# Fourth layer of a four-layer decode step with gradients: resident transposes dealt out between arriving w1 tiles and into two normalisations, twelve zero stores moved to the end

## The chip, the cores and the metric

The kernel runs on one core of a Trainium2 chip. The metric is device time in microseconds (us) of one execution. Engines are named as in the profile: PE (TensorE matmul), PEld (TensorE weight load), DVE (VectorE), ACT (ScalarE), POOL (GpSimd), SP (SyncE, which here only issues DMAs).

## The reference

One token of width 1024 passes four residual layers: attention (A), dense block (B), attention, dense block; A and B have the same weights both times. The outputs are the result of the forward pass and the gradients of all inputs.

```python
def _A_ref(x, k_cache, v_cache, wq, wo):          # 32 query heads, 4 key/value heads, width 128
    W = min(4096, max(256, Sk // 4))              # the last 4096 of 32768 positions
    q = (x @ wq) ...
    k = repeat(k_cache[:, :, Sk - W:, :]); v = repeat(v_cache[:, :, Sk - W:, :])
    p = softmax(q k * Dh ** -0.5)
    return (p v) @ wo

def _B_ref(x, w1, b1, w2):                        # 1024 -> 3584 -> 1024
    h = x @ w1 + b1
    return (h * tanh(softplus(h))) @ w2

x = x + _A_ref(_layernorm(x), ...)
x = x + _B_ref(_layernorm(x), ...)
x = x + _A_ref(_layernorm(x), ...)
x = x + _B_ref(_layernorm(x), ...)
...
_out, _vjp = jax.vjp(_f, A_x, A_k_cache, A_v_cache, A_wq, A_wo, B_w1, B_b1, B_w2)
return (_out, *_vjp(grad_out))
```

The gradients of the two caches have the full 32768 positions, and all but the last 4096 are zero. Writing those zeros is most of the kernel's output: 112 pieces of 128 x 2048 bf16, 0.5 MB each.

## The kernel before

**Stages.** The order of the program is `attn_fwd` (A1), `mlp_B2_fwd`, `attn_fwd` (A3), `mlp_B4`, `ln_bwd`, `attn_bwd` (A3), `mlp_B2_bwd`, `attn_bwd` (A1) and the output jobs. `mlp_B4` is the fourth layer; it does forward and backward in one pass, since the gradient of its output is given. In the profiled execution the layers begin at about 0, 70, 114 and 147 us, the backward of the third at 225, that of the second at 256, that of the first at 306, and the first weight gradients are stored from 329 us on.

**What stays in SBUF.** wq, wo, K and V are loaded once. The forward pass needs them one way round and the backward pass the other way, so each piece of 128 x 1024 has to be transposed in place: eight 128 x 128 transposes on TensorE (L254) into a PSUM bank of the pool `pt` (three banks), then one copy by VectorE or ScalarE (`evac`, L228 and L230; a running estimate of each engine's load picks the engine). Such a piece is a *unit*; there are 88 of them (32 wq, 8 K, 16 V, 32 wo). `unit` lists one as soon as the forward pass is done with it, `fill(n)` transposes the next `n` of the list in the order wo, V, K, wq, and `fill_kind` finishes all of a kind before the product that needs them. Where the fills stand in the program is written out by hand: the lists `F_` of the attention layers, `FB4` of the fourth layer.

**What is streamed.** w1 and w2 pass through rings of SBUF slots. `queue` is the order of all loads; `rel` returns a slot and `pump` issues the next loads that have one. All these loads and all stores but some small ones go through SP's queue, in program order, with eight transfers under way at most. In the third and fourth layer the ring `r4` has four slots, which lie in the half of K that is free after the third layer's scores; they hold one block of w1.

**The fourth layer.** w1 is worked in four blocks of 1024 columns (the last of 512). Block `b` goes through `fwd(b)` (the products of the normalised input with each w1 tile of 0.5 MB as it arrives, into the PSUM tile `big`), one fill, `sel(b)` (column sums, L670), `act(b)` (the activation and its derivative, some fifteen small VectorE operations on 128 x 8), `turn(b)` (the block's own tiles are transposed in place) and `bwd(b)` (products of the hidden gradient with them into `R`; then `rel` of the slots, which issues the next block's loads). Then come the block's zero stores, `zeros(ZB4[b])`, and twelve fills. The next block's first product waits for its tile.

```python
        for b in range(4):
            fwd(b)
            fill(FB4[b][0])
            sel(b)
            act(b)
            turn(b, 0, 8 if b < 3 else 4)
            fill(FB4[b][1])
            bwd(b)
            ...
            zeros(ZB4[b])
            fill(FB4[b][2])
```

**Zero stores.** `zeros(n)` issues the next `n` pieces from a tile of zeros on SP's queue; they wait for nothing but the queue. Before: 4 in the second layer, 33 in the third, 38 in the fourth, 11 and 4 in the backward of the third and second, 7 before the backward of the first, 8 in it, and 7 among the output jobs.

**Output stage.** Weight gradients are outer products of pairs of rows (PE, L237), copied from PSUM to staging tiles of 0.5 MB (DVE L863, ACT L866) and stored from there by SP. There are seven such tiles in turn (nine from the wo jobs on). Jobs are listed by `add(kind, n, f, z)`, where `z` zero stores follow the job: seven pairs of w2 columns, sixteen w1 jobs with the K and V gradients between them, then wo and wq.

Of the kernel before, what the change touches and what calls it, by code (L numbers as in the profile page):

```python
# [14 lines left out]
P = 128  # L15
# [6 lines left out]
def kernel(  # L22
# [22 lines left out]
    nc = tc.nc  # L45
# [202 lines left out]
    def bc(col, n=32):  # L248
        return col.to_broadcast([P, n])
# [17 lines left out]
    def fill(n):  # L267
        for _ in range(min(n, len(units))):
            u = units.pop(0)[2]
            T8(nat_blocks(u), u)  # L270

    def fill_kind(kind):
        fill(sum(u[0] <= rank[kind] for u in units))

# [49 lines left out]
                wt[name] = (1, n, kt([P, wk_n.get(name, n)], FP32, name)[:])  # L324
        return wt[name][2][:, 0:n]

    def ln_fwd(x_col, l):
        xx = wk("xx", 2 * TD)
        nc.vector.tensor_copy(xx[:, 0:TD], x_col[:])
        nc.vector.tensor_mul(xx[:, TD:], x_col[:], x_col[:])  # L330
        sps = sm_tile(P, 2 * TD)
        mm(sps[:], bc(oneD[:, 0:1], P), xx[:], True, True)
        s12 = wk("s12", 2)
        nc.vector.reduce_sum(s12[:], sps[:].rearrange("p (a b) -> p a b", a=2), axis=AX.X)
        var = wk("var", 1)
        nc.vector.scalar_tensor_tensor(out=var[:], in0=s12[:, 0:1], scalar=s12[:, 0:1], in1=s12[:, 1:2],
                                       op0=ALU.mult, op1=ALU.subtract, reverse1=True)
        lnv = wk("lnv", 1)
        nc.scalar.activation(lnv[:], var[:], ACT.Ln, bias=eps_t[:, 0:1], scale=1.0)
        rstd = wk(f"rstd_{l}", 1)  # L340
        nc.scalar.activation(rstd[:], lnv[:], ACT.Exp, scale=-0.5)
        n_bf = npair[:, LI[l], :]
        nc.vector.tensor_scalar(out=n_bf, in0=x_col[:], scalar1=s12[:, 0:1], scalar2=rstd[:, 0:1], op0=ALU.subtract, op1=ALU.mult)
        n32 = kt([P, TD], FP32, f"n32_{l}")
        last = nc.vector.tensor_scalar(out=n32[:], in0=x_col[:], scalar1=s12[:, 0:1], scalar2=rstd[:, 0:1], op0=ALU.subtract, op1=ALU.mult)
        return dict(n32=n32, rstd=rstd, l=l), n_bf, last

    def ln_bwd(tt, sv, g_col, nxt, hook=None):

        n32, rstd = sv["n32"], sv["rstd"]  # L350
        nc.vector.tensor_mul(tt[:, TD:], tt[:, 0:TD], n32[:])
        if hook:
            hook()
        sps = sm_tile(P, 2 * TD)
        mm(sps[:], bc(oneD[:, 0:1], P), tt[:], True, True)
        ab = wk("s12", 2)
        nc.vector.reduce_sum(ab[:], sps[:].rearrange("p (a b) -> p a b", a=2), axis=AX.X)  # L357
        t2 = wk("t2", TD)
        nc.vector.scalar_tensor_tensor(out=t2[:], in0=n32[:], scalar=ab[:, 1:2], in1=tt[:, 0:TD],
                                       op0=ALU.mult, op1=ALU.subtract, reverse1=True)  # L360
        gx = wk("gx", TD)
        nc.vector.tensor_scalar(out=gx[:], in0=t2[:], scalar1=ab[:, 0:1], scalar2=rstd[:, 0:1], op0=ALU.subtract, op1=ALU.mult)
        g_new = kt([P, TD], FP32, f"g_{nxt}")
        g_bf = kt([P, TD], BF16, "gb_X0")[:] if nxt == "X0" else gpair[:, LI[nxt], :]
        nc.vector.tensor_add(g_bf, g_col[:], gx[:])
        last = nc.vector.tensor_add(g_new[:], g_col[:], gx[:])
        return g_new, g_bf, last


# [266 lines left out]
        return x_new, sv, da4  # L636

    def mlp_B4(x_col, da4):
        sv, n_bf, g0 = ln_fwd(x_col, "B4")
        dh = kt([P, TF], FP32, "dh_B4")  # L640
        sv["dh"] = dh
        R = one_tile("R", 512)
        big = one_tile("big", 1024)
        blk, hcol = {}, {}

        def fwd(b):
            full = b < 3
            nh, nt, nch = (2, 2, 4) if full else (1, 4, 2)
            hb = big[:, (b % 2) * 512:(b % 2 + 1) * 512]
            blk[b] = [take(("w1b", b, i)) for i in range(nch)]  # L650
            for i in range(nch):
                w = blk[b][i][0]
                for ti in range(nt):
                    t = nt * i + ti
                    for n in range(nh):
                        g = 2 * n + ti if full else ti
                        mm(hb[32 * g:32 * g + 32, :], bc(n_bf[:, t:t + 1]), w[:, ti, n * 512:(n + 1) * 512],
                           i == 0, i == nch - 1, tile_position=(0, 32 * g))
            evac(jkf[:, :], hb, 512, "D")

        def sel(b):
            full = b < 3
            nh, nk = (2, 8) if full else (1, 4)
            hps = sm_tile(P, 8)
            for cc in range(2):
                for tt in range(2):
                    k = 2 * cc + tt
                    mm(hps[:, k:k + 4 * (nh - 1) + 1:4], jkf[:, cc * 256 + tt:cc * 256 + tt + 255:2], selD[:] if full else sel1[:], k == 0, k == 3)
            h = wk("h", nk)
            nc.vector.tensor_add(h[:], hps[:, 0:nk], b1_f[:, 8 * b:8 * b + nk])  # L670
            hcol[b] = h

        def act(b):
            nk, f0 = 8 if b < 3 else 4, 8 * b
            dact = wk("dact", nk)
            mish(hcol[b][:], apair[:, 0, f0:f0 + nk], dact[:], nk)
            nc.vector.tensor_mul(hpair[:, 0, f0:f0 + nk], da4[:, f0:f0 + nk], dact[:])
            nc.vector.tensor_mul(dh[:, f0:f0 + nk], da4[:, f0:f0 + nk], dact[:])
            spent(2.8, 0.2)

        def turn(b, lo, hi):
            for u in range(lo, hi):
                if b < 3:
                    w = blk[b][u // 2][0][:, u % 2, :]
                    T8([w[:, (k // 2) * 256 + k % 2:(k // 2) * 256 + k % 2 + 255:2] for k in range(8)], w)
                else:
                    w = blk[b][u // 2][0][:, 2 * (u % 2):2 * (u % 2) + 2, :]
                    T8([w[:, q, (k // 2) * 256 + k % 2:(k // 2) * 256 + k % 2 + 255:2] for q in range(2) for k in range(4)],
                       w.rearrange("p t f -> p (t f)"))

        def bwd(b):
            nk, f0 = 8 if b < 3 else 4, 8 * b
            for k in range(nk):
                for tp in range(4):
                    w = blk[b][tp][0][:, 0:2, :] if b < 3 else blk[b][tp // 2][0][:, 2 * (tp % 2):2 * (tp % 2) + 2, :]
                    mm(R[32 * tp:32 * tp + 32, 0:256].rearrange("p (t d) -> p t d", t=2), bc(hpair[:, 0, f0 + k:f0 + k + 1]),
                       w[:, :, k * P:(k + 1) * P], b == 0 and k == 0, b == 3 and k == nk - 1, tile_position=(0, 32 * tp))
            for _, ring, i in blk.pop(b):
                rel(ring, i)
# [9 lines that stand above are left out]
            if b == 3:  # L709
                zsrc[:] = [None, 1024]  # L710
            zeros(ZB4[b])
            fill(FB4[b][2])
        evac(jkf[:, 0:256], R[:, 0:256], 256, "D")
        dn = sm_tile(P, TD)
        for i in range(2):
            mm(dn[:].rearrange("p (a i) -> p i a", i=2)[:, i, :], jkf[:, i * P:(i + 1) * P], ident_f[:, 0:P:32], i == 0, i == 1)
        tt = wk("xx", 2 * TD)
        nc.vector.tensor_copy(tt[:, 0:TD], dn[:])
        return tt, sv
# [282 lines left out]
    def wo_dead():  # L1002
# [42 lines left out]

        for n in range(NW2 // 2):
            add("w2a", n, lambda c=2 * n: pair_half(row_sp["w2"], c, w2_out, w2_lhs, 0))
            add("w2", n, lambda c=2 * n: pair_half(row_sp["w2"], c, w2_out, w2_lhs, 1), {0: 1, 2: 2, 6: 1}.get(n, 0))
        for n in range(16):
            add("w1", n, lambda t=n // 2, hf=n % 2: w1_job(t, hf), n < 3)  # L1050
            add("kv", n, lambda n=n: kv_step(n))
        for n in range(HQ // 8):
            add("wo", n, lambda c=4 * n: tall_jobs(row_sp["wo"], range(c, c + 4), wo_out, wo_lhs))
# [24 lines left out]
    def out_step(i):  # L1078
        if i == 0:
            nc.scalar.copy(z8.bitcast(FP32), zlo[:, 0:2].bitcast(FP32).to_broadcast([P, 2048]))  # L1080
            zsrc[:] = [z8, 4096]
            zeros(8)
        elif i < 3:
            rows_turn(row_sp["w2"], i - 1, w2_sp[i - 1], "rep")
        elif i > 2:
            run_jobs(1 if i == 4 else 2)

    ZB4 = [11, 10, 10, 7]
    FB4 = [(1, 0, 12), (1, 0, 12), (1, 0, 12), (1, 8, 0)]

    pump()
    x1, sA1 = attn_fwd(x0, "A1", True, sA, [0] * 6, [0] * 4)
    x2, sB2, da4 = mlp_B2_fwd(x1)
    x3, sA3 = attn_fwd(x2, "A3", False, sB, [4, 2, 8, 2, 2, 2], [10, 4, 19])
    tt, sB4 = mlp_B4(x3, da4)
    g3, g3b, _ = ln_bwd(tt, sB4, gcol, "A3")
    g2, g2b, _ = attn_bwd(g3, g3b, "A3", sA3, False, "B2", [4, 3, 5, 2], [5, 1, 5], lambda i: None)
    (g1, g1b, _), x4_bf = mlp_B2_bwd(g2, g2b, sB2, x3)
    zeros(7)
    g0, g0b, _ = attn_bwd(g1, g1b, "A1", sA1, True, "X0", [0] * 4, [0, 0, 0], out_step)  # L1100
    assert not queue and not held and not units
    order[:] = ["op", "big0", "big1", "op", "acc", "R", "op", "sm"]
# [37 lines left out]
```

## Time and profile before

| | us |
|---|---|
| three runs | 445.44, 449.69, 450.57 |
| median | 449.69 |
| span of the profiled execution | 446.6 |

| | busy, us | share of the span |
|---|---|---|
| PE | 329.8 | 74% |
| PEld | 195.8 | 44% |
| DVE | 234.5 | 53% |
| ACT | 220.7 | 49% |
| POOL | 14.7 | 3% |
| SP's DMA queue, as a share of 16 engines | | 96.9% |

169.45 MB are moved (70.00 MB read and 98.84 MB written), 379 GB/s on the mean over the span.

How to read what is shown below. The slices cut the span into 40 parts of 11.2 us; digits are tenths, 9 being 90% or more. PEclk is the clock that TensorE was granted, in tenths of full speed. In the table by stretches each row has the stretch, its length, the busy time and number of instructions of PE, PEld, DVE, ACT and POOL, the granted clock, the DMA share (1.02 to 1.05 where all engines are busy throughout) and GB/s. In the order of time each row has the start, the duration, engine and line, output and inputs, and in brackets the idle time of the engine before it and what ended that. The line of a matmul is mostly that of the helper `mm` (L237), so rows are told apart by their tiles. Landing is the end of a DMA's transfer as its semaphore shows it. A busy share of PE says little by itself, since matmuls are pipelined.

### The profile page before, as it was taken

To read this page: it belongs to the slowest core of one execution; us is meant where nothing else is said; L and a number is where in the kernel's file an instruction comes from. 1 tells how busy PE (TensorE), PEld (TensorE's weight loads), DVE (VectorE), ACT (ScalarE), POOL (GpSimd) and SP (SyncE) were. 2 spreads that over 40 slices of the span, in tenths; PEclk is the share of its full clock that TensorE was granted. 3 is DMA by queue.
4 is the path that set the end of the run, shared out by engine and by line. 5 is a ranking of instruction groups with operands and counts; after the bars stand their busy time and mean duration, and the time that the engine had idled before them with its cause. 6 is when DMAs were issued, how large, how long until landed. Compare 5 with 4: busy or idle time off the path is not lost. (4 is left out here: it accounts for less than half of the span.)

```text
span 446.6 us, 9185 instructions
## 1 busy us (share of the span) xinstructions
PE 329.8 (74%) x3732; PEld 195.8 (44%) x3732; DVE 234.5 (53%) x532; ACT 220.7 (49%) x335; POOL 14.7 (3%) x52
## 2 busy tenths in 40 slices
PE   3486645487778886879878788887589889987770
PEld 1164215355455774858756555773322312221110
DVE  2045102097253452535645378572256888888871
ACT  1045000056173452736724267571457678898881
POOL 1000000000000000000000000000400020000000
PEclk9998655579899796978999989666865555555555
DMA  8999999999999999998999999999998699999997
GB/s 328 423 420 418 409 410 379 401 336 328 365 398 406 417 404 381 341 376 290 381 412 405 374 412 336 383 333 358 415 397 356 280 397 403 371 386 413 408 411 319
DMA packets 49143, 169.45 MB, mean 379 GB/s; under 512 B 4784, under 2 KB 5836, under 8 KB 44876
## 3 DMA queue, kind: packets, MB, share of 16 engines
q1 hardware_dynamic: 48784, 168.31, 96.9%
q8 instruction: 29, 0.48, 0.4%
q0 software_dynamic: 256, 0.54, 0.3%
q14 instruction: 14, 0.11, 0.1%
q10 hardware_dynamic: 60, 0.01, 0.0%
HBM read 70.00 MB, written 98.84 MB: 378 GB/s over the span
## 5 line engine op out<-in xcount | busy, mean ns | idle before, releaser
L230 ACT COPY K<-tp 128x1024 bf16<-128x1024 bf16 x58 | 57.3, 1015 | 18.1 <-PE tp L254 16.9
L254 PE MATMUL tp<-ident_bf,K 128*128 128x128 bf16 x656 | 58.3, 258 | 4.8 <-DMA K<-in_B_w_dram 1.7
L237 PE MATMUL op<-wo 2*128 2x512 bf16 (+2 forms) x123 | 56.0, 566 | 2.3 <-ACT V L866 0.7
L254 PEld LDWEIGHTS <-K 128*128 128x128 bf16 x656 | 50.9, 119 | 11.0 <-issue 8.0
L237 PEld LDWEIGHTS <-wo 128*128 128x128 bf16 (+2 forms) x590 | 22.5, 101 | 65.8 <-issue 56.3
L230 ACT COPY wo<-tp 128x1024 bf16<-128x1024 bf16 x32 | 32.6, 1026 | 29.5 <-PE tp L254 27.2
L237 PE MATMUL big<-wo 2*128 2x512 bf16 x82 | 27.5, 590 | 10.2 <-DVE wo L863 4.0
L866 ACT CAST wo<-op 128x512 bf16<-128x512 f32 (+1 forms) x51 | 29.3, 592 | 5.5 <-PE big L237 2.0
L863 DVE CAST wo<-big 128x512 bf16<-128x512 f32 x31 | 21.1, 686 | 11.5 <-ACT wo L866 6.9
L568 DVE CUSTOM_DVE_ANT_0 K<-K,kp 128x1024 bf16<-128x1024 bf16 (+1 forms) x22 | 24.3, 1126 | 5.3 <-PE R L237 2.3
L254 PE MATMUL tp<-ident_bf,wo 128*128 128x128 bf16 x352 | 26.4, 230 | 0.3 <-ACT wo L230 0.2
L866 ACT CAST wo<-big 128x512 bf16<-128x512 f32 x35 | 20.7, 601 | 11.3 <-DVE wo L863 5.8
L228 DVE COPY jk<-R 128x512 f32<-128x512 f32 (+1 forms) x11 | 7.3, 664 | 33.7 <-PE R L237 33.7
L254 PEld LDWEIGHTS <-wo 128*128 128x128 bf16 x352 | 21.7, 102 | 7.2 <-issue 6.4
L237 PE MATMUL acc<-wo 2*128 2x512 bf16 (+1 forms) x41 | 24.3, 592 | 0.0
L230 ACT CAST jk<-big 128x512 bf16<-128x512 f32 x4 | 2.6, 659 | 42.1 <-DVE jk L228 42.1
L228 DVE COPY K<-tp 128x1024 bf16<-128x1024 bf16 x24 | 16.3, 690 | 11.3 <-PE tp L254 11.2
L237 PE MATMUL big<-wq,npair 128*32 128x512 bf16 x128 | 13.4, 553 | 10.0 <-DMA wq<-in_A_wq_dram 8.6
L237 PE MATMUL sm<-wo 2*128 2x512 bf16 (+1 forms) x33 | 19.9, 604 | 1.1 <-DVE cols L357 1.1
L863 DVE CAST wo<-op 128x512 bf16<-128x512 f32 (+1 forms) x32 | 18.4, 600 | 4.1 <-PE big L237 2.0
L237 PE MATMUL R<-wo 2*128 2x512 bf16 (+1 forms) x33 | 19.7, 596 | 0.0
L228 DVE CAST jk<-big 128x512 bf16<-128x512 f32 x4 | 2.8, 712 | 30.9 <-PE big L237 30.9
(269 smaller groups left out, 591.7 us busy)
## 6 DMA issues: line engine op xcount, KB each, us to landing
out_dram<-misc SPq DMA_DIRECT2D x97, 512.0 KB, 10.3
out_dram<-wo SPq DMA_DIRECT2D x37, 512.0 KB, 4.9
K<-in_B_w_dram SPq DMA_DIRECT2D x28, 512.0 KB, 6.9
K<-in_A_k_cache_dram SPq DMA_DIRECT2D x9, 1024.0 KB, 20.5
wq<-in_A_wq_dram SPq DMA_DIRECT2D x8, 1024.0 KB, 10.1
out_dram<-wq SPq DMA_DIRECT2D x8, 1024.0 KB, 8.0
K<-in_B_w_dram SPq DMA_DIRECT2D x16, 448.0 KB, 5.0
out_dram<-wo SPq DMA_DIRECT2D x16, 448.0 KB, 5.1
```

The lines of the kernel that those rows point to most:

```text
L228: return nc.vector.tensor_copy(out_ap, in_ap)
L230: return nc.scalar.copy(out_ap, in_ap)
L237: return nc.tensor.matmul(out_ap, lhsT=lhsT, rhs=rhs, start=start, stop=stop, skip_group_check=True, **kw)
L254: nc.tensor.transpose(ps[:, b * P:(b + 1) * P], ap, ident_bf[:])
L568: return nc.vector.tensor_tensor_reduce(out=w, in0=w, in1=vec, scale=1.0, scalar=0.0, op0=ALU.mult, op1=ALU.add, accum_out=acc_col)
L863: nc.vector.tensor_copy(out_ap, in_ap)
L866: nc.scalar.copy(out_ap, in_ap)
```

## The change

The fills of the fourth layer are dealt out otherwise: `FT4[b][i]` of them stand before the products of block `b`'s tile `i`, and the twelve behind each block go. `fill_ahead(n)` puts the transposes of `n` units into PSUM at a point where the statistics of a normalisation have just been issued to TensorE, and `fill_land` copies them out after the normalisation's vector chain; this is used in the fourth layer's forward and backward normalisation. The third layer has one fill fewer in its first place; the fourth has 45 (with the two normalisations) instead of 48, so four wq units more are left for `fill_kind("wq")` in the third layer's backward pass. Twelve zero stores are moved: five fewer in the third layer, seven fewer in the fourth, three more ahead of the first layer's backward pass, two more in it, four more among the w2 jobs and three more among the w1 jobs.

```diff
+    ahead = []
+
+    def fill_ahead(n):
+        for _ in range(min(n, len(units), 3 - len(ahead))):
+            u, ps = units.pop(0)[2], ptile()
+            for b, ap in enumerate(nat_blocks(u)):
+                nc.tensor.transpose(ps[:, b * P:(b + 1) * P], ap, ident_bf[:])
+            ahead.append((u, ps))
+
+    def fill_land():
+        while ahead:
+            u, ps = ahead.pop(0)
+            evac(u, ps[:])
...
-    def ln_fwd(x_col, l):
+    def ln_fwd(x_col, l, nfill=0):
...
         mm(sps[:], bc(oneD[:, 0:1], P), xx[:], True, True)
+        fill_ahead(nfill)
...
         last = nc.vector.tensor_scalar(out=n32[:], ...)
+        fill_land()
...
-    def ln_bwd(tt, sv, g_col, nxt, hook=None):
+    def ln_bwd(tt, sv, g_col, nxt, hook=None, nfill=0):
...
         mm(sps[:], bc(oneD[:, 0:1], P), tt[:], True, True)
+        fill_ahead(nfill)
...
         last = nc.vector.tensor_add(g_new[:], g_col[:], gx[:])
+        fill_land()
...
-        sv, n_bf, g0 = ln_fwd(x_col, "B4")
+        sv, n_bf, g0 = ln_fwd(x_col, "B4", 2)
...
             for i in range(nch):
+                fill(FT4[b][i])
                 w = blk[b][i][0]
...
             zeros(ZB4[b])
-            fill(FB4[b][2])
...
-            add("w2", n, ..., {0: 1, 2: 2, 6: 1}.get(n, 0))
+            add("w2", n, ..., (1, 1, 2, 1, 1, 1, 1)[n])
...
-            add("w1", n, lambda t=n // 2, hf=n % 2: w1_job(t, hf), n < 3)
+            add("w1", n, lambda t=n // 2, hf=n % 2: w1_job(t, hf), n < 4 or n in (7, 9))
...
-            zeros(8)
+            zeros(10)
...
-    ZB4 = [11, 10, 10, 7]
-    FB4 = [(1, 0, 12), (1, 0, 12), (1, 0, 12), (1, 8, 0)]
+    ZB4 = [8, 8, 8, 7]
+    FT4 = [(0, 0, 0, 0), (6, 2, 2, 2), (6, 2, 2, 2), (5, 4)]
+    FB4 = [(1, 0), (1, 0), (1, 0), (1, 4)]
...
-    x3, sA3 = attn_fwd(x2, "A3", False, sB, [4, 2, 8, 2, 2, 2], [10, 4, 19])
+    x3, sA3 = attn_fwd(x2, "A3", False, sB, [3, 2, 8, 2, 2, 2], [10, 4, 14])
     tt, sB4 = mlp_B4(x3, da4)
-    g3, g3b, _ = ln_bwd(tt, sB4, gcol, "A3")
+    g3, g3b, _ = ln_bwd(tt, sB4, gcol, "A3", nfill=2)
...
-    zeros(7)
+    zeros(10)
```

The first number of the third layer's `F_` is the count of fills between the copies of the query product and the column matmuls (`j_cols`); the last of `[10, 4, 19]` is the zeros issued ahead of its last product, the last before the fourth layer.

More of the change, by code (lines that the diff above doesn't have):

```diff
@@ L1047, in wo_dead @@
             add("w2a", n, lambda c=2 * n: pair_half(row_sp["w2"], c, w2_out, w2_lhs, 0))
-            add("w2", n, lambda c=2 * n: pair_half(row_sp["w2"], c, w2_out, w2_lhs, 1), {0: 1, 2: 2, 6: 1}.get(n, 0))
+            add("w2", n, lambda c=2 * n: pair_half(row_sp["w2"], c, w2_out, w2_lhs, 1), (1, 1, 2, 1, 1, 1, 1)[n])
         for n in range(16):
-            add("w1", n, lambda t=n // 2, hf=n % 2: w1_job(t, hf), n < 3)
+            add("w1", n, lambda t=n // 2, hf=n % 2: w1_job(t, hf), n < 4 or n in (7, 9))
             add("kv", n, lambda n=n: kv_step(n))
```

## The prediction

> **What bounds the kernel now.** I read the page's slices first, then the busy time by stretches, then the order of time in the fourth layer, then the stretches of the output stage.
>
> The slices (40 of 11.2 us: granted TensorE clock, DMA share, bytes moved):
>
> ```profile
> PEclk9998655579899796978999989666865555555555
> DMA  8999999999999999998999999999998699999997
> GB/s 328 423 420 418 409 410 379 401 336 328 365 398 406 417 404 381 341 376 290 381 412 405 374 412 336 383 333 358 415 397 356 280 397 403 371 386 413 408 411 319
> ```
>
> The DMA engines are busy nearly throughout, at 410 to 420 GB/s in the good slices and near 300 in the bad ones. So bytes that are only moved cost nothing in themselves: time is won where the engines idle less and lost where they idle more. One zero store (0.524 MB) takes 1.25 us at 420 GB/s; twelve take 15.0 us.
>
> The fourth layer by stretches (busy us of PE, PEld, DVE, ACT, POOL with counts, then granted clock, DMA share, GB/s). Each cycle is: loads issued, tiles awaited, block worked through, loads issued.
>
> ```profile
> 161.70:168.00 6.30, 6.21 (x97) 5.64 (x97) 4.44 (x7) 3.96 (x4) 0.00 (x0) 1.00 1.02 385
> 168.00:174.40 6.40, 2.20 (x17) 0.45 (x17) 0.22 (x1) 1.01 (x2) 0.00 (x0) 0.69 1.04 361
> 174.40:184.70 10.30, 9.42 (x116) 8.68 (x112) 5.85 (x21) 4.98 (x6) 0.00 (x0) 0.70 1.02 414
> 184.70:191.00 6.30, 6.05 (x97) 5.57 (x96) 3.96 (x6) 4.19 (x5) 0.00 (x0) 1.00 0.81 266
> 191.00:196.00 5.00, 1.98 (x20) 0.42 (x16) 0.69 (x1) 0.77 (x1) 0.00 (x0) 0.83 0.98 353
> 196.00:207.00 11.00, 10.43 (x118) 9.80 (x115) 5.26 (x20) 6.09 (x7) 0.00 (x0) 0.61 0.95 385
> 207.00:213.30 6.30, 6.09 (x96) 5.51 (x96) 4.06 (x6) 4.45 (x5) 0.00 (x0) 1.00 0.83 256
> 213.30:224.00 10.70, 8.92 (x138) 7.42 (x136) 7.45 (x24) 7.44 (x9) 0.00 (x0) 1.00 0.99 375
> ```
>
> TensorE does twelve fills (transposes of resident tiles) right after each block, then waits 5 to 6 us for w1 tiles nearly empty, and afterwards works the block at a clock of 0.70 and 0.61. The same work after 213.30, where no such wait came before, has 1.00.
>
> In order of time (start, us, engine, line):
>
> ```profile
> 161.67 6.30 PE L254 MATMUL tp<-ident_bf,wo 128*128 128x128 bf16 x96
> 161.71 3.43 SPq L181 DMA_DIRECT2D K<-in_B_w_dram  x4
> 165.19 12.69 SPq L150 DMA_DIRECT2D out_dram<-misc  x11
> 170.76 0.62 PE L237 MATMUL big<-K,npair 128*32 128x512 bf16 x4 [1.44 <-DMA K<-in_B_w_dram]
> 173.84 0.62 PE L237 MATMUL big<-K,npair 128*32 128x512 bf16 x4 [0.73 <-DMA K<-in_B_w_dram]
> 175.25 1.87 PE L237 MATMUL sm<-selD,jk 128*128 128x2 f32 x8
> 184.75 2.94 SPq L181 DMA_DIRECT2D K<-in_B_w_dram  x4
> ```
>
> The fill stretch (96 transposes, 6.30 us) gives 0.52 us a fill at full clock. Block 1's tiles stand in SP's queue behind the zeros of the third layer and the last is used 12.1 us after its issue; block 2's last 10.7 us (195.48 after 184.75).
>
> The output stage:
>
> ```profile
> 335.00:339.50 4.50, 4.50 (x42) 1.40 (x40) 2.18 (x4) 3.39 (x6) 0.00 (x0) 0.50 0.71 277
> 348.50:353.00 4.50, 3.14 (x20) 1.04 (x15) 4.10 (x14) 3.24 (x7) 0.00 (x0) 0.50 0.60 239
> 353.00:357.50 4.50, 3.83 (x21) 0.65 (x18) 4.33 (x10) 3.04 (x7) 0.00 (x0) 0.50 0.65 259
> 384.50:389.00 4.50, 4.33 (x32) 1.31 (x25) 4.00 (x7) 3.71 (x8) 0.00 (x0) 0.50 0.82 324
> 402.50:407.00 4.50, 3.77 (x18) 0.72 (x16) 4.45 (x8) 3.98 (x9) 0.00 (x0) 0.50 1.02 404
> ```
>
> Here the DMA engines have holes up to 398 us and none after 402: the end is set by when the stores drain.
>
> **The change, part by part.**
>
> *Zeros leave the front.* Third layer 33 to 28, fourth 38 to 31. With five fewer, the last zero before block 1's loads lands near 162 rather than 168 (issue up to 157.8 plus the median 10.3 us to landing, less 5 x 1.25). But four w1 loads alone are slow: 184.70 to 191.00 moved 266 GB/s, so 2.1 MB need 7.9 us plus a start of about 2 us. I take 10.0 us from issue to last use with an empty queue: block 1 gains 2.1 (bounds 0 and 3.3: the first of block 3's loads landed 4.2 us after its issue, and three more 1.5 us apart, as block 1's were used, make 8.8), block 2 0.7 (0 to 1.9), block 3 with two tiles 0.8 (0 to 1.5). Sum -3.6.
>
> *Fills between the tiles.* Six stay where they were, then two behind each tile: 12 x 0.52 plus four tile steps of 0.4 to 0.6 is 8.3 us, under the 10.0, so they cost nothing while tiles are the later ones; if tiles came in under 8.3 us, fills would be last. What they bring is the clock. At half clock the column sums took 1.87 us against 1.02 for the same eight at 146.06; a fill 1.03 against 0.61; 48 transposes 4.60 us at 176.97 against 3.15 by the fill stretch. That bounds block 1 at 0 to 2.5 and block 2 likewise; as evacuations (0.69 us VectorE, 1.01 ScalarE) pace part of it, I take 1.4 and 1.8. Sum -3.2.
>
> *Two fills in each normalisation.* Forward, TensorE idles 1.41 us before 149.47; two fills need 1.05 to 1.2: free, and the clock, which fell at 150 for block 0, may hold: -1.0 (0 to -1.5). Backward the hole is 1.06 us: 0 (to +0.3). The evacuations come after the vector chain, so only the next block's 0.69 us copy could queue behind them.
>
> *Counts.* One fill fewer after the third layer's queries: the fourth waited 0.89 us for a PSUM bank and held the column matmuls until 124.11, though their input stood at 122.70: -1.1 (-0.5 to -1.4). The last block has four fills fewer; its twelve (four of its own tiles, eight fills) took 7.7 us (215.62 to 223.29), 0.64 each: -2.6 (-2.1 to -2.6). Four wq units are thus left over and run in front of the next layer's last big product, where six already stand bare (245.22 to 248.38): 4 x 0.52 = +2.1.
>
> *Second layer backward.* Its seventh w2 tile came 1.65 us late (266.19), behind five zeros; with the queue some 10 us ahead that wait goes: -1.5 (0 to -1.65).
>
> Front: -3.6 -3.2 -1.0 -1.1 -2.6 +2.1 -1.5 = **-10.9 us**. Check: the front loses 15.0 us of transfers, so 4.1 us more of idle DMA time must appear there, as holes of 1 to 2 us after each block.
>
> *Zeros at the end.* Ten instead of seven and ten instead of eight before the outputs, four more among the w2 stores, three more among w1's. SP issues in order, so the first w2 stores queue behind five more zeros (6.2 us), and seven staging tiles come free later. What is absorbed: the holes below 1.02 between 326 and 398 add up to 4.5 x (0.11+0.31+0.42+0.37+0.20+0.10) = 6.8 us; by bytes, 367 GB/s from 329.3 to 402 against the 413 that the tail sustains gives 8.1. I take 7.4: 15.0 - 7.4 = **+7.6 us** (6.9 to 15.0, the latter if nothing is absorbed).
>
> Sum: -10.9 + 7.6 = -3.3 us on a profiled span of 446.6. The runs' median is 449.69, 0.7% above that span and inside their own spread; taken off it, **446.4 us**.
>
> **Rivals.**
>
> *The clock does not hold.* If TensorE still falls to 0.5 while it waits, -3.2 and -1.0 are gone: +0.9, 450.6 us. For: the first tile may come 4 to 6 us after issue and six fills last 3.1. Against: the stretch 222.5 to 227 held 1.00 with 2.38 of 4.5 us busy.
> [...]
>
> *Tiles come fast and every hole fills.* Loads at their better bound (another -3.1) and 8.1 us absorbed (-0.7): -7.1, 442.6 us. For: w1 landings pace at 1.3 to 1.8 us behind zeros. Against: 256 and 266 GB/s where they stood alone.
>
> *The staging ring stalls (slower).* The eighth use of a seven-tile ring, in the fourth pair of w2 columns near 338.9 us, needs the first store landed; it did at 333.4 and, 6.2 us later, would at 339.6. From there each further zero puts stores later than the pairs that need their tiles; VectorE and ScalarE are at 8.2 to 9.2 of 10 us between 360 and 400 and cannot catch up, so the holes reappear later instead of filling. At worst nothing is absorbed: -10.9 + 15.0 = +4.1; with loads gaining nothing either, +7.7: 453.8 to 457.4 us. It decides once the first w2 store lands after 339 and shares under 0.9 are still seen beyond it. Against: a stall caused by a full DMA queue leaves that queue full.
>
> That the change is not what it says is excluded by the counts: 112 zeros and 88 units both ways.
>
> **How the numbers follow.** Forecast 0.45, own range 443 to 450.5; clock 0.17; fast tiles 0.20; ring 0.18. A change under 1% (4.5 us: 445.2 to 454.2) is no more than a measurement of this kernel can tell. Faster: 0.18 of the fast rival and a third of the forecast, 0.34. Slower: most of the ring rival and a little of the clock's, 0.19. Same: 0.47. Range 440.5 to 454.5, which leaves out the ring's worse end and the fast rival's tail.
>
> **What would show it.** Granted clock near 1.00 from 150 to 210 us; fourth layer some 11 us shorter with DMA holes after each block's loads are issued; ten wq transposes before the next layer's last product; shares of 1.0 from 300 us to the end. It is wrong if the layer shrinks by under 6 us, or the output stage grows by over 10.

## The result, and the profile after

| | before | after |
|---|---|---|
| median, us (20 runs each) | 449.00 | 451.57 |
| ratio, 95% interval | | 1.0074 [1.0046, 1.0101] |
| span of the profiled execution, us | 446.6 | 450.6 |
| fourth layer, normalisation to normalisation | 77.9 | 67.6 |
| first layer's backward begins | 305.5 | 299.7 |
| from there to the end | 141.1 | 151.0 |

Runs more than 1.5% above the fastest of the same kernel are left out of the ratio, which is therefore not quite the quotient of the two medians (2.6 us apart). By the ratio the change costs 0.7%, some 3.3 us, where 3.3 us of gain was forecast. A span is some 1.8 us shorter than the time of the same run. The layer that the change works on became 10.4 us shorter. The slices of the profile after (granted clock, DMA share, GB/s):

```profile
PEclk9999555588698999998999796957865555555555
DMA  8999999999999969889999899989999999999995
GB/s 334 424 420 415 411 408 374 409 345 338 350 406 418 415 193 389 297 323 368 378 403 382 314 368 319 367 304 403 425 418 419 416 407 408 401 407 412 411 412 234
```

The clock is high from the 14th slice to the 22nd, where before had a 6 and two 7s, and the shares from 300 us on are full. But the bytes that left the fourth layer left holes there: 193, 297 and 323 GB/s in slices 15, 17 and 18, which had 404, 341 and 376 before.

The fourth layer by stretches (length; PE, PEld, DVE, ACT, POOL busy with counts; granted clock, DMA share, GB/s):

```profile
161.35:165.15 3.80, 3.02 (x49) 2.80 (x49) 2.07 (x3) 2.54 (x3) 0.00 (x0) 1.00 0.65 215
165.15:171.00 5.85, 4.50 (x66) 3.30 (x66) 2.32 (x4) 2.23 (x3) 0.00 (x0) 1.00 1.01 330
171.00:180.30 9.30, 7.15 (x113) 5.99 (x112) 5.32 (x21) 6.18 (x8) 0.00 (x0) 1.00 0.95 383
180.30:189.60 9.30, 7.22 (x113) 6.05 (x112) 4.45 (x7) 4.05 (x4) 0.00 (x0) 1.00 0.84 270
189.60:198.80 9.20, 7.58 (x118) 6.13 (x118) 6.04 (x22) 5.79 (x7) 0.00 (x0) 1.00 1.00 407
198.80:203.50 4.70, 2.54 (x41) 2.33 (x41) 1.98 (x3) 1.93 (x2) 0.00 (x0) 0.98 0.71 196
203.50:217.70 14.20, 11.38 (x146) 9.62 (x146) 7.01 (x26) 7.91 (x9) 0.00 (x0) 0.89 1.02 383
```

Blocks 1 and 2 run at full clock throughout, in 19.0 and 18.5 us instead of 23.0 and 22.2. At each issue of loads (161.35, 180.30, 198.80) the DMA share falls to 0.65 to 0.84. The last block has lost the clock (0.89, with 0.50 from 203.3 to 206.7 us).

TensorE in order of time, block 1 and then block 3 (start, us, line, tiles, idle before and what ended it):

```profile
165.18 0.40 PE L237 MATMUL big<-K,npair 128*32 128x512 bf16 x4 [0.66 <-DMA K<-in_B_w_dram]
165.52 1.07 PE L254 MATMUL tp<-ident_bf,wo 128*128 128x128 bf16 x16
...
169.22 0.40 PE L237 MATMUL big<-K,npair 128*32 128x512 bf16 x4 [1.31 <-DMA K<-in_B_w_dram]
...
170.55 0.40 PE L237 MATMUL big<-K,npair 128*32 128x512 bf16 x4
...
172.00 1.10 PE L237 MATMUL sm<-selD,jk 128*128 128x2 f32 x8 [0.50 <-DVE jk L228]
...
203.54 0.62 PE L237 MATMUL big<-K,npair 128*32 128x512 bf16 x4 [2.00 <-DMA K<-in_B_w_dram]
204.09 3.20 PE L254 MATMUL tp<-ident_bf,V 128*128 128x128 bf16 x32
207.21 0.40 PE L237 MATMUL big<-K,npair 128*32 128x512 bf16 x4
...
208.66 1.10 PE L237 MATMUL sm<-sel,jk 128*128 128x1 f32 x8 [0.50 <-DVE jk L228]
```

In block 1 two fills (1.07 us) fit in between tiles, which are used 3.8 to 9.2 us after their issue; the column sums take 1.10 us, not 1.87. In block 3 it goes wrong. Only two tiles come; TensorE idles 2.00 us for the first, the clock drops to 0.50, and then four fills stand between it and the second: 32 transposes in 3.20 us. The second tile had landed at 205.3 and is used at 207.21.

The output stage, in the stretches shown of before:

```profile
335.00:339.50 4.50, 4.09 (x28) 0.90 (x28) 3.50 (x7) 3.39 (x6) 0.00 (x0) 0.50 1.02 416
348.50:353.00 4.50, 3.54 (x20) 0.67 (x20) 4.29 (x12) 2.35 (x6) 0.00 (x0) 0.50 1.02 416
353.00:357.50 4.50, 3.85 (x25) 0.98 (x22) 3.97 (x12) 3.18 (x7) 1.36 (x3) 0.50 1.02 417
384.50:389.00 4.50, 4.27 (x28) 1.13 (x25) 3.34 (x6) 4.48 (x10) 0.00 (x0) 0.50 1.02 405
```

Shares of 0.60 to 0.82 have become 1.02: every hole is filled. Two of the costliest groups show whose wait it is now (us busy, mean ns, idle before, what ended most of it):

```profile
L884 ACT CAST wo<-op 128x512 bf16<-128x512 f32 (+1 forms) x51 | 29.6, 595 | 12.1 <-DMA out_dram<-wo 6.9
L881 DVE CAST wo<-op 128x512 bf16<-128x512 f32 (+1 forms) x32 | 18.4, 598 | 10.2 <-DMA out_dram<-wo 8.8
```

Before, these groups idled 5.5 and 4.1 us and waited for TensorE:

```profile
L866 ACT CAST wo<-op 128x512 bf16<-128x512 f32 (+1 forms) x51 | 29.3, 592 | 5.5 <-PE big L237 2.0
L863 DVE CAST wo<-op 128x512 bf16<-128x512 f32 (+1 forms) x32 | 18.4, 600 | 4.1 <-PE big L237 2.0
```

Now they wait for a staging tile to be stored.

### The profile page after: what moved, and what is told of

Read it like the earlier page. It is cut to its first block, busy times and chain, and to the rows that moved or that the text cites. A ratio compares the mean times of both kernels' runs of the same rounds, so it can differ in the third digit from the quotient of the medians.

```text
span 450.6 us, 9186 instructions
## 1 busy us (share of the span) xinstructions
PE 323.9 (72%) x3732; PEld 188.6 (42%) x3732; DVE 233.7 (52%) x532; ACT 220.0 (49%) x335; POOL 14.5 (3%) x52
## 5 line engine op out<-in xcount | busy, mean ns | idle before, releaser
L254 PE MATMUL tp<-ident_bf,K 128*128 128x128 bf16 x656 | 51.3, 235 | 9.5 <-ACT K L230 3.7
L230 ACT COPY wo<-tp 128x1024 bf16<-128x1024 bf16 x33 | 33.6, 1024 | 34.2 <-PE tp L254 30.6
L254 PEld LDWEIGHTS <-K 128*128 128x128 bf16 x656 | 43.1, 106 | 16.8 <-issue 11.5
L884 ACT CAST wo<-op 128x512 bf16<-128x512 f32 (+1 forms) x51 | 29.6, 595 | 12.1 <-DMA out_dram<-wo 6.9
L237 PE MATMUL big<-wo 2*128 2x512 bf16 x82 | 26.4, 578 | 11.6 <-DVE wo L881 4.7
L881 DVE CAST wo<-big 128x512 bf16<-128x512 f32 x31 | 21.1, 685 | 13.6 <-ACT wo L884 7.2
L254 PE MATMUL tp<-ident_bf,wo 128*128 128x128 bf16 x336 | 25.1, 228 | 0.3 <-ACT wo L230 0.3
L228 DVE COPY jk<-R 128x512 f32<-128x512 f32 (+1 forms) x11 | 7.3, 665 | 33.3 <-PE R L237 33.3
L254 PEld LDWEIGHTS <-wo 128*128 128x128 bf16 x336 | 20.2, 102 | 7.4 <-issue 7.4
L237 PE MATMUL big<-wq,npair 128*32 128x512 bf16 x128 | 14.2, 591 | 10.0 <-DMA wq<-in_A_wq_dram 8.6
L228 DVE COPY wo<-tp 128x1024 bf16<-128x1024 bf16 x19 | 12.8, 688 | 13.1 <-PE tp L254 13.1
## 6 DMA issues: line engine op xcount, KB each, us to landing
out_dram<-misc SPq DMA_DIRECT2D x88, 512.0 KB, 10.6
```

What stands on the lines that cost most here:

```text
L228: return nc.vector.tensor_copy(out_ap, in_ap)
L230: return nc.scalar.copy(out_ap, in_ap)
L237: return nc.tensor.matmul(out_ap, lhsT=lhsT, rhs=rhs, start=start, stop=stop, skip_group_check=True, **kw)
L254: nc.tensor.transpose(ps[:, b * P:(b + 1) * P], ap, ident_bf[:])
L881: nc.vector.tensor_copy(out_ap, in_ap)
L884: nc.scalar.copy(out_ap, in_ap)
```

## The experiments

A difference in ratio is given in us at 0.01 = 4.5 us. All ratios are to the kernel before, with their 95% intervals, and rest on 10 to 12 runs of a kernel (six of the one with old fills and moved zeros). Each kernel has one profile. Lengths of stages and blocks are read in it between marks: the points where the statistics of a normalisation are reduced or a block's loads are issued.

**The two halves of the change apart.** First the new fills with the zeros where they were (`ZB4 = [11, 10, 10, 7]`, `[10, 4, 19]`, and the old counts at the end):

> The new fills with the old places of all 112 zeros. Theory S (starved front: with zeros gone from the third and fourth layer the DMA engines run dry there, because a block needs about 18.5 us whatever is left out, and every zero not paid for by a shorter layer is paid at the end): the fills by themselves are a gain, as the clock holds at 1.00 through the blocks and the zeros keep the queue full; 3 to 5 us faster than before (ratio 0.989 to 0.994), fourth layer 4 to 6 us shorter, bytes in it about 375 GB/s or more. Rival F (the fills are what costs: the last block lost 2.0 us between its loads' issue and its column sums, and four wq units stand bare later): 1 to 4 us slower than before (ratio 1.002 to 1.009).

Measured: 0.9956 [0.9918, 0.9993], a gain of 2.0 us and less than the 3 to 5 of theory S. The layer is 3.1 us shorter (74.9 for 77.9 us), and the clock did not hold (0.86 in block 1). Behind the zeros in their old places the first tile of block 1 is awaited for 4.80 us, and the fills between the tiles then run at half clock (1.89 us for sixteen transposes, 1.07 in after):

```profile
168.40 0.62 PE L237 MATMUL big<-K,npair 128*32 128x512 bf16 x4 [4.80 <-DMA K<-in_B_w_dram]
168.95 1.89 PE L254 MATMUL tp<-ident_bf,wo 128*128 128x128 bf16 x16
```

Block 1 takes 23.9 us (23.0 before). Then the old fills with the twelve zeros moved:

> The old fills with the twelve zeros moved. S: tiles come 2.9 and 1.5 us sooner in blocks 1 and 2, but TensorE still waits and still falls to half clock, so the fourth layer shrinks by 3 to 5 us only, against 7 to 10 us more after 300 us: 4 to 6 us slower than before (ratio 1.009 to 1.014), slower than fills and zeros together. F: the zeros are neutral or a gain and the fills cost: within 1 us of before or faster (ratio at most 1.002).

Measured: 1.0121 [1.0068, 1.0174], as S said. The two multiply to 1.0076, as the change itself: the halves do not interact by any amount that shows, though the intervals leave some 3 us either way. The fills gain 2.0 us; the zeros cost 5.4.

**What the zeros cost at the end and bring in front.** Three kernels leave the twelve zeros out altogether, so that twelve pieces of the cache gradients stay unwritten. The kernel before:

```diff
-    ZB4 = [11, 10, 10, 7]
+    ZB4 = [8, 8, 8, 7]
...
-    x3, sA3 = attn_fwd(x2, "A3", False, sB, [4, 2, 8, 2, 2, 2], [10, 4, 19])
+    x3, sA3 = attn_fwd(x2, "A3", False, sB, [4, 2, 8, 2, 2, 2], [10, 4, 14])
```

> The kernel before with the twelve zero stores taken out of the third and fourth layers as in the change (five and seven), and not issued anywhere else: twelve pieces of the cache gradients are left unwritten. It gives what the front gains by their absence alone, by medians and not by one profile. Theory S, by the marks of the profiles so far: the front gains about 2 us (first layer's backward normalisation at 303.5 where it was 305.5), and the end costs 9 to 10; so 0.9955 of before, 0.992 to 0.999. Rival, the forecast's own terms: loads -3.6 and the seventh w2 tile -1.5, -5.1 us, 0.989 or less. A second rival: the front is bound by transfers after all, and the time falls by most of the twelve's 15 us, 0.975 or less.

Measured: 0.9949 [0.9910, 0.9988], -2.3 us. The kernel after, with the old counts at the end:

```diff
-            add("w2", n, ..., (1, 1, 2, 1, 1, 1, 1)[n])
+            add("w2", n, ..., {0: 1, 2: 2, 6: 1}.get(n, 0))
-            add("w1", n, ..., n < 4 or n in (7, 9))
+            add("w1", n, ..., n < 3)
-            zeros(10)
+            zeros(8)
...
-    zeros(10)
+    zeros(7)
```

> The changed kernel without its twelve additional zero stores at the end (7, 8, four among the w2 jobs and three among w1's, as before); the same twelve pieces are left unwritten. After against this is the price of twelve zeros at the end. Theory S: 9 to 10 us, of which some 2 lie in the last transfers; so this comes at 0.985 to 0.988 of before. Rival, the forecast: the price is 7.6 us and the front's gain 10.9, 0.976. If the price is near 15 us (0.974), the output stage absorbs nothing, and if it is under 6 (0.994), the front's gain is what was overestimated and nothing is wrong with the end's term.

Measured: 0.9918 [0.9880, 0.9956], -3.7 us. So twelve zeros at the end cost 1.0074 - 0.9918, 7.0 us (4.9 to 9.1 by the two intervals); with the old fills 1.0121 - 0.9949, 7.7 us. My theory, taken from the marks of single profiles (9 to 10 us), was too high; the forecast's 7.6 stands. The whole front, fills and zeros, is worth 3.7 us and not 10.9. Some 73 us from the first output jobs on, without the twelve and with them (the first row from this kernel, the second from after):

```profile
321.40:394.00 72.60, 65.00 (x392) 17.92 (x392) 57.97 (x118) 57.57 (x112) 4.42 (x17) 0.50 0.95 377
```

```profile
322.00:395.00 73.00, 60.64 (x379) 17.54 (x372) 54.49 (x112) 53.69 (x103) 4.43 (x17) 0.53 1.02 412
```

The stage absorbs what it has room for: 35 GB/s more over 73 us is 2.6 MB of the 6.3 MB. The rest, 3.7 MB or 9 us at 410 GB/s, stays over; the runs put the price at 7.0.

**The clock by itself.** The kernel before, with sixteen identity transposes whose output nothing reads ahead of each tile of blocks 1 and 2; they keep TensorE busy and move nothing else.

```diff
+                if b in (1, 2):
+                    for _ in range(2):
+                        ps = ptile()
+                        for k in range(8):
+                            nc.tensor.transpose(ps[:, k * P:(k + 1) * P], ident_bf[:], ident_bf[:])
                 w = blk[b][i][0]
```

> The kernel before with sixteen transposes of the identity, which nobody reads, ahead of each tile's products in blocks 1 and 2; nothing else. They keep TensorE at work while tiles are awaited. If the clock is what the dealt-out fills bring, the granted clock stays at 1.00 there, the stretch from the last tile's use to the release shrinks from 10.9 and 11.5 us to 9.3 to 9.8, and the kernel is 2 to 3.5 us faster than before (ratio 0.992 to 0.996). Rival: the fills-only kernel gained by fewer fills in the layer and other places; then sixteen useless transposes a tile change nothing or cost up to 1 us (ratio 1.000 to 1.003).

Measured: 0.9994 [0.9952, 1.0037]. By stretches (the profiled execution, 449.8 us, is one of this kernel's longest, so only the blocks are read):

```profile
170.40:176.90 6.50, 5.99 (x88) 4.51 (x87) 0.80 (x3) 0.92 (x1) 0.00 (x0) 1.00 1.01 376
176.90:184.90 8.00, 6.44 (x105) 5.56 (x106) 5.16 (x21) 4.88 (x6) 0.00 (x0) 1.00 1.03 418
...
205.60:228.00 22.40, 18.89 (x239) 16.71 (x238) 12.49 (x34) 11.99 (x13) 0.00 (x0) 0.84 0.96 340
```

The clock does hold while tiles are awaited (1.00 in blocks 1 and 2), and from the last tile's use to the release blocks 1 and 2 take 9.13 and 9.12 us where before had 10.91 and 11.48. But the last block, reached that much earlier, waits 1.76 us for a tile, falls to half clock (1.87 us for the column sums, 1.10 in block 2; 0.84 on the mean of the block) and takes 22.4 us instead of 19.1. So the clock and the blocks came out as the first reading said, and the total did not: no gain is seen, with some 2 us left open either way. The same with the zeros gone, the same twelve pieces unwritten:

> The unread identity transposes ahead of each tile of blocks 1 and 2 again, now with the twelve zero stores gone as in the two kernels above (the same twelve pieces unwritten), so that no zeros of the third layer stand ahead of the loads. In the earlier run with them the granted clock held at 1.00 from 156 to 214 us and the two cycles from release to release went from 23.0 and 22.2 to 20.9 and 20.7 us, but it fell in block 3 instead (214 to 221) and the total did not move. Theory S, the clock is worth something only where the time freed is not lost to the next wait: against the run without the transposes 0 to -1 us, a ratio to before within 0.003 of it. Rival, the clock was worth its 3.7 us and the queue of zeros hid it: 0.008 below it.

Measured: 0.9956 [0.9917, 0.9995], against 0.9949 without the transposes: nothing, as S said. Here the probe reaches its limit. With tiles coming earlier the unread transposes are themselves last: blocks 1 and 2 take 20.55 and 20.7 us at a clock of 1.00, where the kernel without them took 19.05 and 21.05 at 0.91 and 0.84. What a held clock is worth to the total is thus known only for the late tiles of before, and there, by the one profile, it is lost again in the next wait.

**The last block.** The changed kernel with all nine fills ahead of the block's first tile:

```diff
-    FT4 = [(0, 0, 0, 0), (6, 2, 2, 2), (6, 2, 2, 2), (5, 4)]
+    FT4 = [(0, 0, 0, 0), (6, 2, 2, 2), (6, 2, 2, 2), (9, 0)]
```

> The changed kernel with the nine fills of the last block all ahead of its first tile (9, 0) instead of (5, 4). If the last block's 2.0 us went to four fills that stood behind tile 0 at half clock, its second tile is used 1.5 to 2.5 us sooner after the issue of its loads (6.3 to 7.0 us instead of 8.4) and the kernel is 1.5 to 2 us faster than the changed one (ratio to before 1.003). If that time went to the loads themselves, the second tile is used within 0.5 us of now and the time stays.

Measured: 1.0027 [0.9990, 1.0064], 2.1 us under the change itself (0.0 to 4.2 by the two intervals). TensorE in order of time:

```profile
204.44 0.40 PE L237 MATMUL big<-K,npair 128*32 128x512 bf16 x4
205.75 0.40 PE L237 MATMUL big<-K,npair 128*32 128x512 bf16 x4 [0.91 <-DMA K<-in_B_w_dram]
...
206.94 1.10 PE L237 MATMUL sm<-sel,jk 128*128 128x1 f32 x8 [0.24 <-DVE jk L228]
```

The loads are issued at 199.55, the second tile is used 6.2 us later and the sums begin after 7.39 us; in after it is 8.4 and 9.84.

**The normalisations.** From the version with both edits below, without the fills there (two more go into block 0, two more into the last block):

```diff
-        sv, n_bf, g0 = ln_fwd(x_col, "B4", 2)
+        sv, n_bf, g0 = ln_fwd(x_col, "B4", 0)
...
-    FB4 = [(1, 0), (1, 0), (1, 0), (1, 4)]
+    FB4 = [(3, 0), (1, 0), (1, 0), (1, 6)]
...
-    g3, g3b, _ = ln_bwd(tt, sB4, gcol, "A3", nfill=2)
+    g3, g3b, _ = ln_bwd(tt, sB4, gcol, "A3", nfill=0)
```

> As the kernel with both edits, but no fills in the two normalisations; two more after the first block's products and two more in the last block's turn. If those fills are free where they stand, taking them out costs 0.5 us a fill, 1.5 to 2.5 us in all, with the stretch from the fourth layer's statistics to the first release at 12 us or more instead of 11.2; if they only stand in for others, the time stays within 1 us.

Measured: 1.0014 [0.9978, 1.0050] against 0.9931 with them: 3.7 us (1.6 to 5.9), more than the 1.5 to 2.5 expected. Block 0's first product without the fills, and with them:

```profile
152.61 1.13 PE L237 MATMUL big<-K,npair 128*32 128x512 bf16 x16 [1.41 <-DVE npair L358]
```

```profile
150.58 1.90 PE L237 MATMUL big<-K,npair 128*32 128x512 bf16 x16 [0.51 <-DVE npair L358]
```

The hole is used, and block 0 is 1.0 us shorter (12.08 for 13.06 us, which holds the two fills placed there instead), though the product itself took 1.90 us for 1.13. The remainder of the 3.7 has no place in the two profiles.

**Zeros into the new holes.** Six of the twelve go back where after has holes (three into the third layer, two into block 0's place, one into block 1's; the expectation's "eight" miscounts):

```diff
-    ZB4 = [8, 8, 8, 7]
+    ZB4 = [10, 9, 8, 7]
...
-    x3, sA3 = attn_fwd(x2, "A3", False, sB, [3, 2, 8, 2, 2, 2], [10, 4, 14])
+    x3, sA3 = attn_fwd(x2, "A3", False, sB, [3, 2, 8, 2, 2, 2], [10, 4, 17])
...
-            add("w2", n, ..., (1, 1, 2, 1, 1, 1, 1)[n])
+            add("w2", n, ..., (1, 1, 1, 1, 0, 1, 0)[n])
...
-    zeros(10)
+    zeros(7)
```

> The changed kernel with eight zeros moved back: three into the third layer's last group, two and one into the first two blocks, where the DMA engines stood idle for 4.5, 1.9 and 1 us, and three from ahead of the first layer's backward pass and three from the w2 jobs taken out. S: six zeros (7.5 us) leave the saturated end, whose holes then reopen by 2 to 3 us, and the front grows by at most 1.5 us: 3 to 5 us faster than the changed kernel, ratio to before 0.996 to 1.001. F: the zeros do not matter much: within 1 us of the changed kernel (ratio 1.005 to 1.010).

Measured: 0.9950 [0.9918, 0.9981], 5.6 us under the change and a little more than S said. The slices:

```profile
DMA  8999999999999999997999989999999899999997
GB/s 334 425 416 417 411 410 377 402 345 361 328 398 407 417 358 368 380 405 251 420 402 397 376 308 360 363 339 363 419 421 414 358 389 402 404 405 414 409 412 320
```

The 193, 297 and 323 of after are 358, 380 and 405 (the 19th slice fell to 251, where after has 368), the layer is still 68.0 us long, and the output stage keeps only one hole (358). With the last block's edit as well:

> Both earlier edits together: six zeros back in the front's holes and the last block's nine fills ahead of its first tile. If the two are independent, 0.9950 x 1.0027 / 1.0074 = 0.990 of before, some 4.5 us faster; column sums of the last block 7.4 us after its loads' issue and no stretch after 300 us under 0.95 DMA share. If the gain of the last block is only kept where the end is saturated, 0.995.

Measured: 0.9931 [0.9900, 0.9962], 444.91 us, 3.1 us under before: the lowest ratio of the kernels that write all outputs. It lies between the two readings, and its interval reaches both; nor is it apart from the six zeros alone (0.9950) or the new fills alone (0.9956) by more than the intervals. Four wq units more in its last block (`(1, 8)` for `(1, 4)`), so that they don't run in front of the next layer's product:

> As the kernel with both edits, but eight fills instead of four in the last block's turn, so that six wq units instead of ten stand before the third layer's last product, as in the kernel before. By the terms of the prediction the last block grows by 2.6 us and the bare stretch of wq shrinks by 2.1: 0.5 us slower, the same within the interval. If fills in the turn are hidden by the evacuations there, it is 1 to 2 us faster.

Measured: 0.9986 [0.9943, 1.0028], 2.5 us above the kernel without this edit (0.1 to 4.8), where 0.5 was expected and the rival had 1 to 2 us of gain. Its one profile has a shorter span (441.4 us) than that of any other kernel that writes all outputs, and its twelve runs don't bear that out: a single profile is no verdict here.

## Why the prediction was wrong

The forecast had the sign wrong by its sum: -10.9 in front, +7.6 at the end. The runs give -3.7 and +7.0. **The front failed, the end held.** In the front the two terms of the zeros (-3.6 and -1.5) measured -2.3 together. The five of the fills (-3.2, -1.0, -2.6, -1.1, +2.1, -5.8 in all) measured -2.0 with all zeros in place (-3.7 to -0.3) and -1.4 with the twelve gone (-3.8 to +1.1). The step that failed is the adding up: each term took the length of one wait or one slow stretch in one execution and counted it in full as time of the whole kernel. Three terms brought nothing that shows: the last block's -2.6, the third layer's -1.1 and the w2 tile's -1.5, 5.2 of the 7.2 us that are missing. Step by step, with the one profile of each kernel and the runs:

| term of the forecast | us | found |
|---|---|---|
| zeros leave the front: w1 loads, seventh w2 tile | -3.6, -1.5 | together -2.3 by the runs without them (-0.5 to -4.0) |
| clock in blocks 1, 2 | -3.2 | -3.4: last tile to release 9.76 and 9.28 us, before 10.91 and 11.48 |
| block 0 through the normalisation | -1.0 | -2.4: 11.2 us instead of 13.6 (with these fills 11.2 in two profiles, 12.1 to 12.2 in five) |
| last block, four fills fewer | -2.6 | about 0 (18.9 us, before 19.1); -2.1 comes when the fills are put right |
| third layer, one fill fewer | -1.1 | the wait went; the stage is no shorter |
| four wq fills bare | +2.1 | +1.35: 30.13 us for 28.79, both at a clock of 1.00 |
| end | +7.6 | +7.0 or +7.7 by the runs |

*The layer's total* was right by luck. The terms that lie in the fourth layer add up to -10.4 us, and the profile has -10.4. But block 0 and blocks 1 and 2 gave 2.4 and 7.8 us where 1.0 and 6.0 were said, and the last block 0.2 where 3.4 was (its fills and its loads). Outside the layer -0.5 was said, and the profile has +4.3: third layer +1.8, its backward +1.3, the second's +1.2.

*Loads and clock.* In the layer these steps came true: blocks 1 and 2 lost 4.1 and 3.7 us, near the forecast of 3.5 and 2.5. From issue to the last tile's use block 1 took 9.2 us, where 10.0 was estimated; so of the rival "tiles come fast and every hole fills" only the second half came true, and that at the end. The rival "the clock does not hold" is out for the change as a whole; with the zeros in their old places it came true, as the first tile was used 8.0 us after its issue and the six fills ahead of it ended after 3.2. In after the last block fell to half clock (0.50 from 203.3 to 206.7 us) at the end of a gap of 2.00 us, and block 1, whose longest gap was 1.31 us, kept its clock (1.00).

*The last block* is the clearest miss. The step counted twelve transposes by 0.64 us and took four away behind `act`, but it forgot that the same change puts four of the nine tile fills behind the first of only two tiles. They held the second tile back for 2 us and made the column sums late (9.84 us after the issue of the loads, before 7.81) by as much as the part from there to the release gained (-1.9). This is a fill standing where the forecast said it costs nothing "while tiles are the later ones", and there the tile was not.

*The seventh w2 tile.* The wait named did go. The waits of that product for w2 tiles, before and after (us, times):

```profile
  DMA K<-in_B_w_dram: 1.7, 1
```

```profile
  DMA K<-in_B_w_dram: 1.9, 4
```

One wait of 1.65 us became four short ones. The five zeros in front of it are still there; the seventh load is issued 14.2 us after the first of them, before 11.2. The new fills with all zeros in place had four such waits too, 2.5 us in all, so it isn't the twelve zeros that decide. The stage took 51.9 us after, 51.1 in the kernel before without the zeros, 50.7 before, and 49.1 to 52.5 in the other profiles: nothing was won, and what sets its length stays open. The step treated a wait as the price of what stood ahead in the queue, and did not ask what the next tile would do.

*The third layer.* The bank wait went as said. Before, the fourth fill waited ahead of the column matmuls:

```profile
123.67 0.61 PE L254 MATMUL tp<-ident_bf,wq 128*128 128x128 bf16 x8 [0.89 <-ACT wq L230]
124.11 0.36 PE L237 MATMUL acc<-ident_bf,jk 128*128 128x4 bf16 x8
```

In after they follow the fills at once:

```profile
122.43 1.51 PE L254 MATMUL tp<-ident_bf,wq 128*128 128x128 bf16 x24
123.78 0.40 PE L237 MATMUL acc<-ident_bf,jk 128*128 128x4 bf16 x8
```

The stage took 35.1 us all the same, 33.2 before. Its length goes with the time that it spends at half clock (worked out from the mean clock of the stage), and that varies between the profiles, with the old fills as with the new:

| kernel | third layer, us | of that at half clock |
|---|---|---|
| before | 33.2 | 3.4 |
| before without the twelve | 33.3 | 3.4 |
| last block mended | 34.0 | 6.8 |
| new fills, old zeros | 34.1 | 6.8 |
| after | 35.1 | 9.7 |
| old fills, zeros moved | 35.5 | 9.3 |
| six zeros back | 35.5 | 10.6 |

The other six profiles have 34.0 to 36.0 us with 6.8 to 10.1. The profile of before is at the short end. The forecast read one execution as the stage's length; a term of 1.1 us lies inside this scatter of 2.8.

*The check* said that 4.1 us more of idle DMA time must appear in front. From the third layer's normalisation to the first layer's backward the profile after is 6.0 us shorter with twelve zeros less to move, 15.0 us of transfer; so by the bytes 9.0 us more are idle. That the check was the front's gain turned round, and not a bound of its own, is why it warned of nothing.

*The end.* It grew by 9.9 us between the two profiles, just short of the "over 10" that was to show the forecast wrong; that is chance, as the runs put it at 7.0 to 7.7. The first w2 store landed 34.5 us after the beginning of the first layer's backward (27.8 before), past the rival's mark, which was at 33.5. So the staging ring did stall (8.8 and 6.9 us in the groups above), but as was argued, with the DMA queue full: all slices from there on but the last have a share of 0.9 or more. The rival is out: the end cost what the sum of the zeros said, and no more for the ring.

What stays open: which part of the 2 us between the front's profile (-5.8) and its runs (-3.7) is the choice of execution, where the fills lose what the layer gains, and where most of the 3.7 us of the normalisations lie.

## What to carry to other kernels

Where DMA engines are the common bound, transfers moved out of a stage pay only as far as the stage gets shorter than what they took. Here 15 us of stores left the front, which was 2.3 us faster for it, and the end had room for half of them; putting six of the twelve into the holes turned +0.7% into -0.5%. Work dealt out between arriving tiles must be counted against the arrival of each tile, and where one is short of tiles, put ahead of the first. A wait that ends last is worth only the distance to the next one.

## What the runs showed of the hardware that was not expected

In the clock records of before and after TensorE has 1.00 or 0.50, and between two changes lie 3.41, 6.83, 10.24 us and further multiples of 3.41, up to 58.0. With the unread transposes the fall was only moved to the next wait (1.00 in blocks 1 and 2, 0.84 in the last). The third layer took 33.2 to 33.3, 34.0 to 34.3 and 35.1 to 36.0 us with about one, two and three times 3.41 us at half clock, by the mean clock of each. Block 0 took 11.2 and 12.1 to 12.2 us with none and one (new fills), 12.4 to 12.6 and 13.6 with one and two (old fills). The third layer's backward with the old fills took 28.8, 30.1 to 30.3 and 31.6 us with none, one and two. So 3.41 us at half clock go with some 0.9 to 1.5 us of the chain.

In after, where all slices from 304 us on but the last have a share of 0.9 or more, the last transfers straggle: 3.6 us at a share of 0.03. The end of after and of before, by stretches:

```profile
444.00:447.00 3.00, 0.00 (x0) 0.00 (x0) 0.00 (x0) 0.00 (x0) 0.00 (x0) 0.50 0.52 216
447.00:450.60 3.60, 0.00 (x0) 0.00 (x0) 0.00 (x0) 0.00 (x0) 0.00 (x0) 0.50 0.03 14
```

```profile
440.00:443.50 3.50, 0.00 (x0) 0.00 (x0) 0.00 (x0) 0.00 (x0) 0.00 (x0) 0.50 1.00 415
443.50:446.50 3.00, 0.00 (x0) 0.00 (x0) 0.00 (x0) 0.00 (x0) 0.00 (x0) 0.50 0.15 63
```

In the trace of before five of the eight semaphores of SP's queue were raised 592 times for 37 transfers or 576 for 36, so a transfer is counted in sixteen parts. For SP's stores of 0.5 and 1 MB issued between 354 and 414 us, the last part came 3.2 to 3.6 us behind the eighth in after, and 0.1 to 1.9 us in before. A share of 0.03 of sixteen engines is half of one by estimate, which fits a single straggler. Why one falls behind was not tried, and the version with both edits ends in the same way in its profile (0.03 in its last 3.0 us).
